# An H3 layer with a long convolution and an MLP on one core: v fetched in the layout of the transform, and a rearranged first MLP chunk

## The chip, the core and the metric

The kernel runs on one core of a Trainium2 chip. A core has TensorE (PE; PEld is its weight load), VectorE (DVE), ScalarE (ACT), GpSimd (POOL) and the DMA queues, most of which SyncE (SP) fills here. Time is device microseconds for one execution. One execution is also taken with the hardware profiler; its trace is what "the profile" means below.

## The reference

S = 2048 positions, D = 640 channels, F = 1728, all float32. `mod` is six vectors of 640 from `silu(c) @ w_mod`.

```
h  = layernorm(q) * (1 + ca) + sa
kv = causal_conv4(k, shift_k) * v              # per channel, four taps
y  = irfft(rfft(kv, 2S) * rfft(ssm_k, 2S))[:S] + kv * ssm_D
x  = q + ga * (h * y)
h  = layernorm(x) * (1 + cb) + sb
out = x + gb * (relu(h @ w1 + b1)**2 @ w2 + b2)
```

The long convolution is per channel, over 4096 points. kv is the only place where v is used.

## The kernel before, in words

The channels are five blocks (b = 0 to 4) of 128. The Fourier transform is done by matmuls: a position n is 64 n + i, with 32 values of n and 64 of i; the tile `pt[b]` holds, for 32 groups g of four channels, x (slot 0, the product kv) and the filter h (slot 1) with (channel within the group, n) on the 128 partitions and i along the row. `unit_a` (L355) transforms over n, `spectrum` (L362) over i, `front` multiplies the spectra on DVE and combines them on POOL, `back` (L422), `unit_t` (L485) and `unit_y` (L496) transform back.

For kv the positions of a channel must lie along a row, while k and v lie in memory with the channels along a row. So `kv_load` fetches k and v in quarters h of 512 positions (rows of 512 bytes) into the tile KV, `kv_k` transposes k on PE (L221) and scales it on ACT (L222), `kv_s` adds the other three taps on DVE (L233), `kv_v` transposes v on PE (L243), `kv_m` multiplies the two on DVE (L250) and writes the result to the scratch tensor `kv_d` in DRAM (L251). `load_x` reads it back in the layout of the transform (L198), `load_h` the filter (L190).

The order of the work is written out by hand: block b has ten front steps FS(b, j) and 18 (the last block 11) back steps GS(b, s); a table says which small functions run after which step, and every engine and queue runs its instructions in the order in which they are written. While block b goes through its steps, the blocks behind it are prepared: kv of block b + 1 or b + 2, the weight rows `wm` of `mod` (L302, scaled on ACT at L306, added on POOL), q's columns `xp` (L444). SP's queue holds all these loads in the same order, and one that waits holds up those behind it. `unit_a(b + 1, 0, ...)`, the x units of the next block, begin at GS(b, 6), for block 1 at GS(0, 10).

After the convolution comes the MLP in eight chunks of 256 positions (n), each in 14 slices f of the hidden width: `mlp_front` (L664), relu and bias on ACT (L696), the square on POOL (L136), `mlp_split` into a high and a low part on ACT and DVE (L131, L142), and three slices later `mlp_back` (L734). During the first chunk `beside(f)` also loads the weights, splits them into high and low parts on ACT and DVE, and ends the statistics of the second layer norm (`stats2`); `gate_rows` (L1142) fetches b2 as a row and multiplies it on POOL by gb. `keep_order` fixes the order of each engine's instructions; what is written after it may be reordered by the scheduler. It is called after the first chunk's slices.

Of the kernel before, what the change touches and what calls it, by code (L numbers as in the profile page):

```python
# [87 lines left out]
def ssm_mlp_kernel(  # L88
# [91 lines left out]
    hsrc = ssm_k.rearrange("(g a) (n i) -> (a n) g i", a=4, i=64)  # L180
    xsrc = kv_d.rearrange("(g a) (n i) -> (a n) g i", a=4, i=64)
# [4 lines left out]

    def load_h(b, n=1):
        w = DG // n
        for i in range(n):
            sp.dma_start(  # L190
                pt[b][:, 1, i * w : (i + 1) * w],
                hsrc[:, b * DG + i * w : b * DG + (i + 1) * w, :],
            )

    def load_x(b, n=1):
        w = DG // n
        for i in range(n):
            sp.dma_start(  # L198
                pt[b][:, 0, i * w : (i + 1) * w],
                xsrc[:, b * DG + i * w : b * DG + (i + 1) * w, :],  # L200
            )
# [12 lines left out]
    def kv_k(b, h, tag="Y"):  # L214
        acc = KACC[h % 2] if b else K0[:, h]
        t = kt[0] = ps.tile(
            [P, 512], F32, tag=tag, name=f"kt_{b}_{h}", bufs=4 if tag == "X" else 2
        )
        kn = KN[h % (4 if b == 0 else 2)]
        for j in range(4):  # L220
            pe.transpose(t[:, j * P : (j + 1) * P], kn[:, 0, j], ident)  # L221
        act.activation(acc, t, AF.Copy, scale=tap[:, b, 0:1])  # L222
        if h < 3:
            copy(act, ktail[:, h % 2, 0:3], t[:, 509:512])

# [11 lines left out]
    def kv_v(b, h, tag="X"):  # L237
# [6 lines left out]
        n = 4 * b + h + 2  # L244
        if 6 <= n < 4 * NB:
            kv_load(n)

    def kv_m(b, h):
        acc = KACC[h % 2] if b else K0[:, h]
        dve.tensor_mul(acc, kt[1], acc)  # L250
        sp.dma_start(kv_d[b * P : (b + 1) * P, h * 512 : (h + 1) * 512], acc)  # L251

# [236 lines left out]
    def unit_y(b, g):  # L489
# [13 lines left out]
        if g % 2:  # L503
            uo = UPt[b][:, :, 16 * (g - 1) : 16 * (g + 1)].rearrange("p l (g d) -> p g l d", d=4)
# [94 lines left out]
    def stats2(l0, l1):  # L599
        for l in range(l0, l1):  # L600
            dve.bn_aggr(mv2[:, l], st2[:, l])
        s = slice(l0, l1)
# [24 lines left out]
    def prep_xt(n, b):  # L627
        if b == 0:
# [12 lines left out]
        )  # L641
        copy(act, XT[n][:, 0, b], f)
# [129 lines left out]
    for a in range(4):  # L772
        (pool if a % 2 else act).dma_start(
            dsm[32 * a : 32 * a + 1, :],
            ssm_D.rearrange("(o g a) -> a o g", a=4, o=1)[a],
        )
    act.dma_start(tap, shift_k.rearrange("(b p) t -> p b t", p=P))
    act.dma_start(cw, cw_d.rearrange("p (r m) -> p r m", r=2))
    act.activation(rs1[:, 0:1], eps_t, AF.Copy)
# [4 lines left out]
    def load_h0(i):  # L784
        sp.dma_start(pt[0][:, 1, 8 * i : 8 * i + 8], hsrc[:, 8 * i : 8 * i + 8, :])
# [14 lines left out]
    unit_a(0, 1, 1)  # L800
    kv_all(1)
    load_gb(1)
    unit_a(0, 1, 2)
    unit_a(0, 1, 3)
    kv_all(2)
# [6 lines left out]
    for i in (2, 3):  # L812
        load_gb(i)
# [4 lines left out]
    for i in range(2):  # L818
# [3 lines left out]
        early_h(0, 2 * i + 1)  # L822
    act.dma_start(ct, c.rearrange("o (b p) -> p (o b)", p=P))
# [23 lines left out]
    def put_kv(b, places, tags="YYYY"):  # L847
        for h, p4 in enumerate(places):
            at(p4[0], kv_k, b, h, tags[h])
            for i, fn in zip(p4[1:], (kv_s, kv_v, kv_m)):  # L850
                at(i, fn, b, h)

# [3 lines left out]
    for j in range(4):  # L856
# [4 lines left out]
        [FS(0, i) for i in (1, 2, 3, 4)],  # L861
        [FS(0, i) for i in (5, 6, 7, 8)],
        [GS(0, i) for i in (0, 1, 1, 2)],
        [GS(0, i) for i in (3, 4, 4, 5)],
    ], "TTYX")
    at(GS(0, 6), load_x, 1, 4)
    at(FS(1, 8), load_x, 2)
    at(GS(1, 16), load_x, 3)
    at(GS(2, 16), load_x, 4)
# [3 lines left out]
        [GS(0, i) for i in (8, 9, 10, 11)],  # L873
        [GS(0, i) for i in (12, 13, 14, 15)],
        [FS(1, i) for i in (0, 1, 2, 3)],
        [FS(1, i) for i in (4, 5, 6, 7)],
    ], "XYTT")
    for b in (3, 4):
        at(GS(b - 2, 0), p_tile, b)
        put_kv(b, [[GS(b - 2, 4 * h + i) for i in range(4)] for h in range(4)])  # L880
        at(GS(b - 2, 1), load_h, b)

# [127 lines left out]

    at(FS(4, 4), gate_load)
    at(GS(4, 5), gate_vector)
# [126 lines left out]
    row1b = sb.tile([P, D], F32, tag="row1", name="gb2row")  # L1139

    def gate_rows():
        sp.dma_start(row1b, b2.rearrange("(o d) -> o d", o=1).to_broadcast([P, D]))  # L1142
        mul(pool, row1b, row1b, row0b)

    def residual(n, i, eng):
        add(eng, X1t[n][:, i], X1t[n][:, i], row1b)

    def beside(f):
        n = min(len(stage), len(ahead) + 2 * f)
        while wn[0] < n:  # L1150
# [9 lines left out]
        if f == 2:  # L1160
            stats2(2, 4)
# [4 lines left out]
        if f in (6, 7, 8):  # L1166
            stats2(4 * f - 20, 4 * f - 16)
        if f == 9:
            stats2_end(4, NL)
        if f == 4:  # L1170
            gate_rows()
# [3 lines left out]
    for i in range(len(seq) + MLAG):  # L1175
# [9 lines left out]
        if i <= last:  # L1185
# [5 lines left out]
            if n == 0:  # L1191
                beside(f)
            if n + 1 < NC:
# [4 lines left out]
                if f >= 8 and f - 8 < NB:  # L1198
                    prep_xt(n + 1, f - 8)
# [28 lines left out]
```

## Time and profile before

| | us |
|---|---|
| median of three timed runs | 727.67 (726.03 to 729.06) |
| the profiled execution | 725.62 |
| its span in the trace | 723.8 |
| prologue until the first x unit of block 0 | 0 to 30.9 |
| convolution with its preparation | 30.9 to 313 |
| MLP, first chunk | 313 to 370 |
| MLP, seven further chunks and the tail | 370 to 723.8 |

The span is the part of the execution that the trace covers; some 2 us lie around it. In a row of the timeline stand the start, the length, the engine, the line, the operation, the tile that is written and those that are read, the count, and in brackets the engine's idle time just before and what ended it. In a row of groups stand the busy time, the mean length and the idle time.

### The profile page before, as it was taken

The page shows a single profiled execution, that of the slowest core. Times are in us where ns is not written, and L with a number is a line of the kernel's source. Part 1 is how long each engine was busy: PE and PEld are TensorE (multiplying, and loading weights), DVE is VectorE, ACT ScalarE, POOL GpSimd, SP SyncE. Part 2 cuts the span into 40 slices and gives each one's busy share as a digit, 9 for nine tenths or more (in the row PEclk, how much of TensorE's full clock was granted, in tenths as well). Part 3 has the DMA queues.
Part 4 walks back from the last instruction along what each step waited for, and adds up shares of the span by engine and source line. Part 5 has one row for each costly group of instructions (what it writes and reads, how often), then busy time and mean ns, then how long its engine had stood idle before and what let it go on. Part 6 is the DMA issues. An engine that isn't in the chain of part 4 may idle for free.

```text
span 723.8 us, 18538 instructions
## 1 busy us (share of the span) xinstructions
PE 694.8 (96%) x7916; PEld 660.5 (91%) x7916; DVE 339.3 (47%) x665; ACT 333.4 (46%) x688; POOL 289.5 (40%) x337
## 2 busy tenths in 40 slices
PE   5899999989999999998999999999999999999996
PEld 5788898879899889887899999999999999999996
DVE  3455674576868779676751231232232312322312
ACT  3535565576885876455543323332333233233221
POOL 1033036147846968733363333342342333243211
PEclk9999999999999999999999999999999999999998
DMA  9697685986355473326401020020020010200001
GB/s 222 180 222 242 165 272 152 266 268 163 103 168 147 108 185 122 118 65 180 137 16 58 1 72 3 1 74 1 1 73 1 37 37 1 74 1 1 38 1 38
DMA packets 88563, 72.62 MB, mean 100 GB/s; under 512 B 19552, under 2 KB 74272, under 8 KB 88480
## 3 DMA queue, kind: packets, MB, share of 16 engines
q1 hardware_dynamic: 86176, 70.83, 34.6%
q8 instruction: 62, 1.02, 0.6%
q10 hardware_dynamic: 2240, 0.60, 0.4%
q14 instruction: 21, 0.17, 0.1%
q0 software_dynamic: 64, 0.00, 0.0%
HBM read 57.01 MB, written 14.42 MB: 99 GB/s over the span
## 4 chain that ended last, share of the span: by engine, by line
PE 81%; DVE 6%; ACT 4%; issue 4%; DMA 3%; POOL 2%; ACTq 0%; DVEq 0%; POOLq 0%; SPq 0%
PE acc L734 24%; PE h L664 22%; PE pa L355 8%; PE x L362 5%; PE y L496 4%; PE qp L422 4%; PE h L362 4%; PE t L485 2%; PE kt L221 1%; PE h L655 1%; PE vt L243 1%; PE xtp L632 1%; DMA wx<-in_cw_dram 1%; DVE KV L233 1%; DVE w_S L142 1%
## 5 line engine op out<-in xcount | busy, mean ns | idle before, releaser
L664 PE MATMUL h<-xt,w_S 128*128 128x256 f32 x1290 | 167.1, 281 | 0.1
L734 PE MATMUL acc<-w_S,hring 128*128 128x320 f32 x960 | 159.4, 314 | 4.6 <-ACT hring L131 3.6
L664 PEld LDWEIGHTS h<-xt,w_S 128*128 128x128 f32 x1290 | 161.5, 190 | 0.3 <-DVE w_S L142 0.3
L142 DVE TENSOR_TENSOR hring<-mtmp,hring 128x256 fp32r<-128x256 f32 x112 | 63.1, 563 | 196.8 <-ACT hring L131 196.8
L136 POOL TENSOR_TENSOR mtmp<-mtmp 128x256 f32<-128x256 f32 x112 | 72.8, 650 | 201.7 <-ACT mtmp L696 186.7
L734 PEld LDWEIGHTS acc<-w_S,hring 128*128 128x128 f32 x960 | 142.9, 189 | 6.9 <-ACT hring L131 4.2
L696 ACT ACTIVATE mtmp<-h,b1t 128x256 f32<-128x256 f32 x104 | 48.9, 471 | 131.1 <-PE h L664 128.1
L131 ACT ACTIVATE hring<-mtmp 128x256 fp32r<-128x256 f32 x112 | 46.7, 417 | 89.2 <-POOL mtmp L136 89.2
L355 PE MATMUL pa<-wx,p 128*64 128x128 f32 x1280 | 83.7, 280 | 3.8 <-DMA wx<-in_cw_dram 2.7
L355 PEld LDWEIGHTS pa<-wx,p 128*64 128x64 f32 x1280 | 70.4, 139 | 10.7 <-issue 7.8
L131 ACT ACTIVATE a<-pa 128x512 f32<-128x512 f32 x80 | 47.7, 599 | 26.5 <-PE pa L355 26.5
L136 DVE TENSOR_TENSOR wx<-x,wx 128x512 f32<-128x512 f32 x64 | 40.9, 683 | 21.0 <-ACT wx L131 8.6
L496 PE MATMUL y<-wx,wx 128*64 128x64 f32 x1280 | 44.6, 223 | 3.1 <-ACT wx L131 2.4
L496 PEld LDWEIGHTS y<-wx,wx 128*64 128x64 f32 x1280 | 41.3, 138 | 6.6 <-ACT wx L131 3.5
L233 DVE SCALAR_TENSOR_TENSOR KV<-kt,tap,KV 128x511 f32<-128x511 f32 (+2 forms) x48 | 35.6, 742 | 20.7 <-ACT ktail L131 19.4
L634 DVE TENSOR_SCALAR we<-xtp,cbs 128x256 f32<-128x256 f32 x35 | 19.0, 542 | 55.0 <-PE xtp L632 55.0
L142 POOL TENSOR_TENSOR we<-wx 128x256 f32<-128x256 f32 x20 | 15.7, 783 | 72.1 <-DVE wx L136 67.3
L139 POOL TENSOR_TENSOR wm<-wm,wm 128x640 f32<-128x640 f32 x20 | 31.8, 1590 | 31.2 <-ACT wm L306 31.1
L362 PE MATMUL x<-a,gb 128*64 128x128 f32 x640 | 41.7, 273 | 0.7 <-ACT a L131 0.7
L142 POOL TENSOR_TENSOR xt<-we,xt 128x256 fp32r<-128x256 f32 x35 | 25.7, 735 | 36.0 <-ACT xt L131 36.0
L362 PEld LDWEIGHTS x<-a,gb 128*64 128x64 f32 x640 | 35.9, 137 | 1.7 <-ACT a L131 0.9
L131 ACT ACTIVATE q<-qp 128x512 f32<-128x512 f32 x39 | 21.2, 595 | 34.8 <-PE qp L422 34.8
(143 smaller groups left out, 1040.0 us busy)
## 6 DMA issues: line engine op xcount, KB each, us to landing
wm<-in_w_mod_dram SPq DMA_DIRECT2D x25, 320.0 KB, 4.8
KV<-in_A_k_dram SPq DMA_DIRECT2D x20, 256.0 KB, 6.0
KV<-in_A_v_dram SPq DMA_DIRECT2D x20, 256.0 KB, 4.3
xp<-in_A_q_dram SPq DMA_DIRECT2D x5, 1024.0 KB, 8.4
out_dram<-x SPq DMA_DIRECT2D x14, 320.0 KB, 2.2
w1s<-in_B_w_dram SPq DMA_DIRECT2D x13, 320.0 KB, 3.7
w2s<-in_B_w_dram SPq DMA_DIRECT2D x13, 320.0 KB, 4.1
kv_d<-KV SPq DMA_DIRECT2D x16, 256.0 KB, 4.1
```

The lines of the kernel that those rows point to most:

```text
L131: act.activation(o, i, AF.Copy)
L136: eng.tensor_mul(o, a, b)
L139: eng.tensor_add(o, a, b)
L142: eng.tensor_sub(o, a, b)
L233: dve.scalar_tensor_tensor(o, x, tap[:, b, t : t + 1], o, op0=ALU.mult, op1=ALU.add)
L355: pe.matmul(t[64 * r : 64 * r + 64, u], w, cw[:, r], start=True, stop=True)
L362: pe.matmul(t[64 * a : 64 * a + 64, s + r], gb[:, g, r, a], AX[b][i][:, 2 * g + a], start=True, stop=True,)
L422: pe.matmul(t[a][:, u], gi[l, 4 * j + u, r], w[r][l, u % 2], start=(r == 0), stop=(r == 1),)
L496: pe.matmul(y[64 * h : 64 * h + 64, 4 * (g % 2) + i], tss[g][:, i, 64 * r : 64 * r + 64], ca[:, r, h], start=(r == 0), stop=(r == 1),)
L664: pe.matmul(hps[n, f][:m], WI[1, f][:, a, b], XT[n][:, x, b], start=(b == 0 and i == 0), stop=(b == NB - 1 and i == 2),)
L696: act.activation(r[:m], h[:m], AF.Relu, bias=b1t[:m, f : f + 1])
L734: pe.matmul(acc[2 * s + i], h[:, a, s * P : (s + 1) * P], w[:, y, i * 320 : (i + 1) * 320], start=(f == 0 and ti == 0), stop=(f == NF - 1 ...
```

## The change

1. For blocks 1 to 4, v is no longer transposed and no longer multiplied before `kv_d`: `kv_d` holds the convolved k alone, `kv_v` is gone for these blocks, and `kv_m` only writes. `v_load` fetches v in four parts j of 16 values of i per block, four DMAs each, in pieces of 32 channels (128 bytes) straight into the transform's layout, into the half of KV where v was; block 1 has four slots, later blocks two. `x_mul` multiplies the tile p by it on DVE, for blocks 2 to 4 one product per part j, before the x units.
2. So that 32 neighbouring channels share a partition row, the channels of a group are now 32 apart in blocks 1 to 4: `by_channel` loads h and x with four DMAs of 32 partitions where one of 128 stood (block 1's x: 16 for four), ssm_D's rows are loaded to match, and y's copy into UP writes with the other stride.
3. The steps in the table move: the taps of kv run a few steps earlier, `load_x` one to three steps earlier, and the v loads and products get steps of their own.
4. Prologue: tap and cw are issued first on ACT; block 0's part of ssm_D goes out from POOL in four pieces, the rest later from ACT; the loads of the table gb stand elsewhere in SP's queue.
5. First MLP chunk: b2's row is loaded at GS(4, 1) and multiplied by gb right after gb's copies; the sums of `stats2` go ahead of the weight splits on DVE, and so do the transposes and scalings of the next chunk's input; `keep_order` is called after the last chunk, so that all chunks run in the written order.

On PE nothing changes but the v transposes and the places of the k transposes among the other matmuls.

```diff
+    def by_channel(src, b, i, dst):
+        w = dst.shape[1]
+        if b == 0:
+            v = src.rearrange("(g a) (n i) -> (a n) g i", a=4, i=64)
+            sp.dma_start(dst, v[:, i * w : (i + 1) * w, :])
+            return
+        for a in range(4):
+            c = b * P + 32 * a + i * w
+            sp.dma_start(
+                dst[32 * a : 32 * a + 32],
+                src[c : c + w, :].rearrange("g (n i) -> n g i", i=64),
+            )
...
-        for w, src in ((0, k), (1, v)):
+        for w, src in ((0, k), (1, v)) if b == 0 else ((0, k),):
             sp.dma_start(t[:, w], src[rows, cols].rearrange("(t p) d -> p t d", p=P))
...
     def kv_m(b, h):
         acc = KACC[h % 2] if b else K0[:, h]
-        dve.tensor_mul(acc, kt[1], acc)
+        if b == 0:
+            dve.tensor_mul(acc, kt[1], acc)
         sp.dma_start(kv_d[b * P : (b + 1) * P, h * 512 : (h + 1) * 512], acc)
+
+    VB = KV[:, 1024:5120].rearrange("p (j w i g) -> p j w i g", j=4, w=2, g=DG)[:, :, 1]
+
+    def v_load(b, j):
+        src = v.rearrange("(n i) d -> n i d", i=64)
+        for a in range(4):
+            c = b * P + 32 * a
+            sp.dma_start(
+                VB[32 * a : 32 * a + 32, j % (4 if b == 1 else 2)],
+                src[:, 16 * j : 16 * j + 16, c : c + 32],
+            )
+
+    def x_mul(b, j):
+        if b == 1:
+            x = pt[b][:, 0, 8 * j : 8 * j + 8].rearrange("p g (j i) -> p g j i", j=4)
+            mul(dve, x, x, VB[:, :, :, 8 * j : 8 * j + 8].rearrange("p j i g -> p g j i"))
+        else:
+            x = pt[b][:, 0, :, 16 * j : 16 * j + 16]
+            mul(dve, x, x, VB[:, j % 2].rearrange("p i g -> p g i"))
...
-            uo = UPt[b][:, :, 16 * (g - 1) : 16 * (g + 1)].rearrange("p l (g d) -> p g l d", d=4)
+            if b == 0:
+                uo = UPt[b][:, :, 16 * (g - 1) : 16 * (g + 1)].rearrange("p l (g d) -> p g l d", d=4)
+            else:
+                uo = UPt[b].rearrange("p l (d g) -> p g l d", d=4)[:, 4 * (g - 1) : 4 * (g + 1)]
...
-    for a in range(4):
-        (pool if a % 2 else act).dma_start(
-            dsm[32 * a : 32 * a + 1, :],
-            ssm_D.rearrange("(o g a) -> a o g", a=4, o=1)[a],
-        )
     act.dma_start(tap, shift_k.rearrange("(b p) t -> p b t", p=P))
     act.dma_start(cw, cw_d.rearrange("p (r m) -> p r m", r=2))
+    for a in range(4):
+        pool.dma_start(
+            dsm[32 * a : 32 * a + 1, 0:32],
+            ssm_D[0:P].rearrange("(o g a) -> a o g", a=4, o=1)[a],
+        )
...
+    put_v(1, [FS(0, i) for i in (3, 4, 6, 7)], [GS(0, i) for i in (8, 9, 10, 11)])
+    at(GS(0, 3), load_x, 1, 4)
+    at(FS(1, 7), load_x, 2)
+    at(GS(1, 15), load_x, 3)
+    at(GS(2, 15), load_x, 4)
...
+    put_v(2, [FS(1, 0), FS(1, 2), FS(1, 9), GS(1, 0)], [FS(1, 9), GS(1, 0), GS(1, 3), GS(1, 4)])
+    put_v(3, [GS(1, 9), GS(1, 11), FS(2, 2), FS(2, 3)], [FS(2, 1), FS(2, 2), FS(2, 6), FS(2, 7)])
+    put_v(4, [GS(2, 9), GS(2, 11), FS(3, 2), FS(3, 3)], [FS(3, 1), FS(3, 2), FS(3, 6), FS(3, 7)])
...
+    def b2_load():
+        row1b[0] = sb.tile([P, D], F32, tag="row1", name="gb2row")
+        sp.dma_start(row1b[0], b2.rearrange("(o d) -> o d", o=1).to_broadcast([P, D]))
...
+    at(GS(4, 1), b2_load)
...
+    mul(pool, row1b[0], row1b[0], row0b)
...
-        if f == 4:
-            gate_rows()
...
-        if i == NF - 1:
-            keep_order()
+    keep_order()
```

(`put_v(b, loads, products)` gives the steps of the four loads and of the four products; in one step the product stands before the load. Before, `load_x` stood at GS(0, 6), FS(1, 8), GS(1, 16) and GS(2, 16).)

More of the change, by code (lines that the diff above doesn't have):

```diff
@@ L224, in kv_k @@
             copy(act, ktail[:, h % 2, 0:3], t[:, 509:512])
+        n = 4 * b + h + 2
+        if b and n < 4 * NB:
+            kv_load(n)
     def kv_s(b, h):
@@ L822, in ssm_mlp_kernel @@
         early_h(0, 2 * i + 1)
+    for a in range(4):
+        act.dma_start(
+            dsm[32 * a : 32 * a + 1, 32:].rearrange("o (c g) -> o c g", g=DG),
+            ssm_D[P:].rearrange("(o c a g) -> a o c g", o=1, a=4, g=DG)[a],
+        )
     act.dma_start(ct, c.rearrange("o (b p) -> p (o b)", p=P))
@@ L1138, in ssm_mlp_kernel @@
     w_tile("KV", 4)
[L1139 to L1143, printed above, removed]
     def residual(n, i, eng):
-        add(eng, X1t[n][:, i], X1t[n][:, i], row1b)
+        add(eng, X1t[n][:, i], X1t[n][:, i], row1b[0])
     def beside(f):
         n = min(len(stage), len(ahead) + 2 * f)
+        if f == 2:
+            stats2_sum(2, 4)
+        if f in (6, 7, 8):
+            stats2_sum(4 * f - 20, 4 * f - 16)
         while wn[0] < n:
@@ L1191, in ssm_mlp_kernel @@
             if n == 0:
+                if f >= 8 and f - 8 < NB:
+                    prep_xt1(n + 1, f - 8)
                 beside(f)
```

69 lines of the change are left out of this document (34 added, 35 removed).

## The prediction

> **What bounds the kernel now.** I read the page's busy line first, then a table of windows that cut the span at its stages. Its columns: length, busy time of PE, PEld, DVE, ACT and POOL with instruction counts, granted PE clock, DMA share, GB/s.
>
> ```profile
> PE 694.8 (96%) x7916; PEld 660.5 (91%) x7916; DVE 339.3 (47%) x665; ACT 333.4 (46%) x688; POOL 289.5 (40%) x337
> ...
> 36.00:96.00 60.00, 58.79 (x966) 51.47 (x963) 36.30 (x78) 30.93 (x58) 11.78 (x18) 1.00 0.81 218
> 96.00:158.00 62.00, 59.33 (x991) 52.75 (x988) 39.96 (x84) 39.52 (x72) 25.50 (x27) 1.00 0.81 231
> 158.00:245.00 87.00, 85.68 (x1455) 78.42 (x1455) 63.25 (x119) 62.74 (x128) 61.06 (x61) 1.00 0.53 144
> 245.00:320.00 75.00, 72.17 (x1221) 65.08 (x1218) 57.15 (x107) 49.09 (x105) 49.77 (x48) 1.00 0.42 120
> ...
> 320.00:369.70 49.70, 44.45 (x308) 41.70 (x307) 35.95 (x69) 25.08 (x53) 19.61 (x20) 0.97 0.48 139
> 369.70:418.80 49.10, 49.10 (x379) 49.10 (x378) 14.01 (x27) 16.94 (x39) 20.60 (x26) 1.00 0.08 28
> ```
>
> The reader is to see two things. From 36 to 320 us, the convolution, PE is busy 275.97 of 284 us: a matmul taken out there is a matmul's time won, if nothing new makes PE wait. From 369.7 us each MLP chunk takes 49.1 us with PE never idle, so nothing is to be won there. The one loose stage in between is the first chunk, idle 49.70 - 44.45 = 5.25 us. The DMA share is 0.81 until 158 us and falls to half after it: that is where more DMA work would hurt.
>
> **The change part by part.**
>
> *v's transposes.* Sixteen groups of four go (blocks 1 to 4; block 0 keeps its own). What one costs PE is the distance to the next instruction's start:
>
> ```profile
> 51.73 0.66 PE L243 MATMUL vt<-ident,KV 128*128 128x128 f32 x4
> 52.32 1.97 PE L362 MATMUL x<-a,gb 128*64 128x128 f32 x32
> ...
> 136.49 0.66 PE L243 MATMUL vt<-ident,KV 128*128 128x128 f32 x4
> 136.98 0.60 PE L485 MATMUL t<-ident,q 128*128 128x128 f32 x4
> ...
> L250 DVE TENSOR_TENSOR KV<-vt,KV x16: 636/677/692, 54.8 to 212.8; 128x512 f32<-128x512 f32 x16
> ```
>
> 0.59 us and 0.49 us, so 16 x 0.49 to 0.59 = 7.8 to 9.4 us; I take **-8.7**. DVE's sixteen products of 512 columns (0.68 us) become sixteen of 512 columns on p's tile: equal in count and size. The new ones read v with a stride of 32 floats, and block 1 to 4's copy of y now writes with such a stride. No row of before shows that stride; between no change and double, 0 to 16 x 0.68 = 11 us of DVE work, beside PE. I take no change, the nearest row. [...]
>
> *The first MLP chunk.* This is the surest term. b2's row is fetched at L1142 behind the weight loads on SP's queue, and POOL, which executes in order, waits for it with the squares of the MLP queued behind:
>
> ```profile
> 333.69 0.42 SPq L1142 DMA_DIRECT2D gb2row<-in_B_b_dram  x1
> ...
> 335.68 1.93 PE L664 MATMUL h<-xt,w_S 128*128 128x256 f32 x15
> ...
> 338.24 1.53 POOL L136 TENSOR_TENSOR gb2row<-gb2row,gbrow 128x640 f32<-128x640 f32 x1 [8.54 <-DMA gb2row<-in_B_b_dram]
> ...
> 340.85 1.10 PE L734 MATMUL acc<-w_S,hring 128*128 128x320 f32 x4 [3.24 <-ACT hring L131]
> ...
> 344.49 1.98 PE L664 MATMUL h<-xt,w_S 128*128 128x256 f32 x15
> ...
> 350.32 0.30 ACT L603 ACTIVATE rs<-mv,eps_t 128x4 f32<-128x4 f32 x1 [2.58 <-DVE mv L601]
> ...
> 376.23 1.95 PE L664 MATMUL h<-xt,w_S 128*128 128x256 f32 x15
> ...
> 379.77 1.94 PE L664 MATMUL h<-xt,w_S 128*128 128x256 f32 x15
> ```
>
> and, from the table of windows, the granted clock right after the stall (the column 0.57):
>
> ```profile
> 341.00:345.00 4.00, 3.75 (x16) 3.35 (x17) 3.67 (x7) 1.70 (x5) 1.61 (x2) 0.57 0.07 15
> ```
>
> From one h group to the next the settled period is 379.77 - 376.23 = 3.54 us; here it is 344.49 - 335.68 = 8.81, so 5.27 us too long: 3.24 idle, most of the rest at a granted clock of 0.57. The change loads the row in the last block and multiplies it before the MLP starts, when POOL has nothing queued. The next thing late is the weight stream (load, high half on ACT, low half on DVE), which kept 3.5 to 4.1 us per f before the stall, so I count **-5.0**. The other moves there (statistics' sums ahead of the weight halves on DVE, the next chunk's transposes ahead of them) cut ACT's waits of the 350.32 kind. What is left to win is the other idle time, 5.25 - 3.24 = 2.0, down to nothing; I take **-1.2**. The order fixed for all chunks moves work on ACT and POOL only, where PE has been busy without a gap: 0, hidden by PE; if that cover fails it shows as idle PE in every chunk.
>
> *The prologue.* ACT now issues tap and cw first:
>
> ```profile
> 1.22 1.26 ACTq L773 DMA_DIRECT2D dsm<-in_A_ssm_D_dram  x2
> ...
> 3.17 0.60 ACTq L778 DMA_DIRECT2D wx<-in_cw_dram  x1
> ...
> 7.89 0.21 POOL L139 TENSOR_TENSOR p<-p,dsm 128x8 f32<-128x8 f32 x1 [5.17 <-DMA dsm<-in_A_ssm_D_dram]
> ...
> 9.45 3.68 PE L355 MATMUL pa<-wx,p 128*64 128x128 f32 x32 [2.73 <-DMA wx<-in_cw_dram]
> ```
>
> cw goes out 1.26 us earlier, but the four pieces of dsm now leave POOL one after another, the last some 1.2 us later than before, and end the wait at about 8.8 us. Four more dsm pieces are issued by ACT ahead of block 0's copies, which costs up to 0.5. Between -1.3 and +0.5; I take **-0.5**.
>
> *v's new loads.* A load of v was 2048 pieces of 512 bytes per block; it is now 8192 of 128 bytes, in 16 DMAs. The rows nearest in kind are the 256-byte loads of h and the 512-byte loads of q (GB/s in forty slices of 43 to 46 us, where h is loaded, and of 244 to 249 us, where q is):
>
> ```profile
> GB/s 225 232 218 218 232 205 246 218 205 218 232 218 205 218 232 218 205 218 232 218 205 218 232 218 205 218 218 218 218 178 178 164 96 96 68 68 68 68 82 55
> ...
> GB/s 102 102 20 102 102 143 164 266 389 397 393 320 283 320 295 233 283 315 348 352 348 348 344 356 336 324 315 283 287 279 299 303 303 283 303 291 279 274 279 312
> ...
> 120.00:158.00 38.00, 35.33 (x611) 31.05 (x608) 22.27 (x50) 27.38 (x51) 10.51 (x8) 1.00 0.91 244
> ```
>
> At 218 GB/s on 16 engines a 256-byte piece takes 256 x 16 / 218 = 18.8 ns of an engine; at about 290, a 512-byte piece 28 ns. A 128-byte piece then costs between 9.4 (by bytes) and 28 ns (as the whole 512-byte row it is cut from); I take 18.8, the nearest size. A block's v is 8192 x 18.8 / 16 = 9.6 us of the engines instead of 2048 x 28 / 16 = 3.6: 6 us more per block, in a queue that is 0.81 to 0.91 full for blocks 1 to 3.
>
> *The new waits.* DVE now multiplies p's tile in order: it waits for x to land, and v's second half may be fetched only when the first products have freed its two slots. For block 2:
>
> ```profile
> 114.70 0.73 DVE L233 SCALAR_TENSOR_TENSOR KV<-kt,tap,KV 128x509 f32<-128x509 f32 x1
> ...
> 119.68 0.34 SPq L251 DMA_DIRECT2D kv_d<-KV  x1
> 122.16 0.69 SPq L198 DMA_DIRECT2D p<-kv_d  x1
> 122.90 4.78 SPq L444 DMA_DIRECT2D xp<-in_A_q_dram  x1
> 127.72 2.30 SPq L302 DMA_DIRECT2D wm<-in_w_mod_dram  x1
> ...
> 135.51 1.05 PE L355 MATMUL pa<-wx,p 128*64 128x128 f32 x16
> ...
> DMA to landing us min/median/max: 3.3/5.7/8.0
> ...
> KV<-in_A_v_dram SPq DMA_DIRECT2D x20, 256.0 KB, 4.3
> ```
>
> (The last two rows: x's loads from issue to landing, and v's, median 4.3.) PE gets to this block's first x unit (135.51 before) about 5.5 us earlier, nine groups and the prologue, at 130. The taps end at 115.4 before, so about 111; the write needs 2.5 us (119.68 to 122.16), so x is asked for at 113.6. Its four loads take SP 4 x 0.69 = 2.8 us, then q's column and a weight row stand in the queue as now (4.78 + 2.30): 123.5. x has landed by about 122 and its first two products free the slots, so eight loads of v follow at some 0.4 us each, until 126.5. Their 4096 pieces need 4.8 us of the engines, so v lands between 123.5 + 4.8 + 2 and 126.5 + 4.3, at 130 to 131, and the last product ends a microsecond later. PE waits 1 to 2.5 us; bounds 0 (9.4 ns a piece) and 6 (28 ns and x at the 8.0 us end). I take **+2.0**. Queued behind DVE's wait are the next block's taps and q's statistics, which have 8 us until PE needs their PSUM buffer.
>
> Block 3 has the same chain with less room, at the start of a block's front:
>
> ```profile
> 157.75 0.38 SPq L251 DMA_DIRECT2D kv_d<-KV  x1
> ...
> 158.49 1.09 PE L362 MATMUL h<-a,gb 128*64 128x128 f32 x16
> ...
> 162.35 1.29 DVE L136 TENSOR_TENSOR wx<-x,wx 128x512 f32<-128x512 f32 x2 [0.46 <-PE x L362]
> ...
> 163.15 0.68 SPq L198 DMA_DIRECT2D p<-kv_d  x1
> ```
>
> Counted from the front's start (158.49), the write goes at -0.7 as now or, without v's product, at -3.4; it needs 5.4 us; x lands 5.7 to 8.0 later, at +7.7 to +12.7. DVE arrives at the product after that of j = 1, at 162.35 + 1.29 - 158.49 = +5.1, and waits 2.6 to 7.6 us with the spectrum products behind it. PE has four PSUM buffers and goes on for some 2.7 us: it loses 0 to 4.9, I take **+1.5**. Block 4's DMA share is half: **+0.5**. Block 1's v is fetched ahead, but its taps move between the front's products on DVE: **+0.5**. ACT and POOL work that waits for weight rows delayed by v: **+1.0**, bounds 0 and 4.
>
> **Sum.** -8.7 - 5.0 - 1.2 - 0.5 = -15.4 of gains; +2.0 + 1.5 + 0.5 + 0.5 + 1.0 = +5.5 of new waits; **-9.9 us**. The profiled execution took 725.62 us (span 723.8), which is below all three timed runs (726.03 to 729.06, median 727.67). So 715.7 on its scale, 717.8 on the median's; I forecast **717.0 us**, nearer to the median's.
>
> **The rivals.** *The cover holds:* v's pieces are cheap and x lands in time; the new waits stay under 1 us in all, 725.6 to 727.7 less 14.5 to 15.4: **about 712**. For it: DVE idles just where block 2's first products stand. Against it: block 3's read is issued 4.7 us after the front starts even now. *The queue fills:* at 28 ns a piece, the 120 to 158 us stage needs 0.91 x 38 = 34.6 us, less five loads of 0.9, plus four of 3.6: 44.5 us of DMA in a stage that PE wants to leave in 36. It runs 8 us late, the gain shrinks to under 2: **about 726**. *The first chunk's wait moves on* to the weight stream and half of that term is lost: **about 720**. *Slower:* one mechanism, the half of v that is fetched on demand. Blocks 2, 3 and 4 each expose 4096 / 16 = 256 pieces per engine between the first product and the last. To end 0.5% slower (3.6 us, about what a measurement of this kernel tells from no change) the three must cost 13 us more than I count, 4.3 each, so 17 ns more a piece: it decides from about 36 ns. At twice the 256-byte row, 37.6 ns, they cost 3 x 4.8 = 14.4 more: **about 732**. Against it: nothing in the trace with pieces of 256 bytes is that slow. [...] The 256-byte rows, at 218 against 290 GB/s, do not show a doubling per piece; no run yet shows 128 bytes.
>
> **How the numbers follow.** Forecast 0.46 (713.5 to 722 on its own), cover holds 0.25, half the first chunk 0.08, the queue fills 0.13, slower 0.08. Faster by over 0.5% (under 724.0) is the first three and a little of the fourth: 0.81; same 0.11; slower 0.08. The range 710 to 726 leaves out the slower rival and the tails.
>
> **What would show it.** Right: no vt groups after block 0; POOL's wait for gb2row gone and the h period near 3.6 us throughout the first chunk, clock 1.00; PE waits of 1 to 4 us at the first x units of block 2 and in the first fronts of blocks 2 and 3 (there x of blocks 3 and 4 is multiplied), released by DVE's product and, behind it, by DMA p or DMA KV. Wrong: a DMA share near 1.0 from 100 to 180 us with wm late on ACT (the queue fills), v's landing times above 8 us, DVE's new product at 1.3 us instead of 0.7, or idle PE in the later chunks.

## The result, and the profile after

The changed kernel takes 737.27 us (median of 4 runs, 735.72 to 740.16) where the kernel before took 728.12 beside it. The ratio over all runs is 1.0134, 95% interval 1.0093 to 1.0176: **slower by 1.3%**. Forecast was 717.0, with a range of 710 to 726. The profiled execution took 740.16 us (span 738.4).

First the busy line of the page and the table of windows, at the same cuts as before (length, busy time of PE, PEld, DVE, ACT, POOL with counts, granted PE clock, DMA share, GB/s):

```profile
PE 694.2 (94%) x7852; PEld 659.6 (89%) x7852; DVE 353.2 (48%) x665; ACT 338.9 (46%) x688; POOL 298.9 (40%) x339
...
36.00:96.00 60.00, 55.52 (x926) 49.25 (x924) 34.51 (x69) 30.40 (x57) 11.74 (x18) 0.97 0.82 179
96.00:158.00 62.00, 54.07 (x900) 47.68 (x897) 41.35 (x84) 35.69 (x65) 22.31 (x25) 1.00 0.96 226
158.00:245.00 87.00, 75.89 (x1229) 68.10 (x1229) 56.01 (x95) 55.59 (x106) 49.10 (x45) 0.92 0.71 147
245.00:320.00 75.00, 69.17 (x1174) 62.62 (x1171) 60.31 (x98) 52.82 (x110) 59.81 (x53) 0.98 0.45 121
320.00:738.40 418.40, 412.74 (x3296) 408.47 (x3295) 146.98 (x292) 148.94 (x325) 152.27 (x186) 1.00 0.14 44
```

PE has 64 matmuls fewer, as planned, yet is busy as long as before (694.2 against 694.8), and idles where it had been full: 29.3 us from 36 to 320, where it was 8.0. The rest of the convolution's loss is the clock column, down to 0.92 in one stage. The whole convolution stands in one pair of windows, from 36 us to the first MLP matmul, before and after.

```profile
36.00:312.68 276.68, 268.88 (x4566) 241.03 (x4562) 193.34 (x380) 178.76 (x352) 145.33 (x149) 1.00 0.64 177
```
```profile
36.00:336.84 300.84, 271.40 (x4490) 241.19 (x4487) 206.40 (x381) 181.69 (x351) 150.28 (x149) 0.97 0.70 162
```

It is 24.2 us longer: 29.4 - 7.8 = 21.6 us more idle, and PE busy 2.5 us more although some 8.7 us of transposes went, so the other matmuls took 11.2 us more. Most of that is the lower clock: added up in windows of 1 us, busy time times the missing part of the clock comes to 8.8 us. After that point the changed kernel gains: 401.6 us to its end where it was 411.1.

The table of PE's waits in this stretch names many releasers and no big one (total, times, longest):

```profile
PE y L523 <- ACT wx L131: 8.4, 3, 5.3
PE y L523 <- ACT up L131: 3.5, 2, 2.2
PE qp L449 <- POOL wx L142: 2.7, 3, 2.2
PE pa L382 <- DVE p L136: 2.5, 1, 2.5
PE y L523 <- DVE KV L242: 2.3, 2, 2.0
PE mr L315 <- POOL wm L139: 2.0, 1, 2.0
PE kt L227 <- issue: 1.8, 1, 1.8
```

Only the fourth is v's product directly. To place the loss by block I use the moment at which ACT copies a block's first q out of PSUM; here the timeline's rows of after:

```profile
107.82 1.08 ACT L131 ACTIVATE q<-qp 128x512 f32<-128x512 f32 x2 [1.96 <-PE qp L449]
...
178.73 1.08 ACT L131 ACTIVATE q<-qp 128x512 f32<-128x512 f32 x2 [2.19 <-PE qp L449]
...
242.97 1.08 ACT L131 ACTIVATE q<-qp 128x512 f32<-128x512 f32 x2 [2.19 <-PE qp L449]
...
301.30 1.09 ACT L131 ACTIVATE q<-qp 128x512 f32<-128x512 f32 x2 [2.05 <-PE qp L449]
```

From one block to the next, in us, read in the same way in every trace (the kernels below are explained with their experiments). A product of a block stands before that block's transform, so stretch 1 to 2 holds block 2's products and the first one or two of block 3's, and stretch 2 to 3 the rest of block 3's and the first of block 4's.

| kernel | ratio to before, 95% | 0 to 1 | 1 to 2 | 2 to 3 | 3 to 4 |
|---|---|---|---|---|---|
| before | 1 | 56.1 | 60.8 | 56.7 | 53.4 |
| after | 1.0134, 1.0093 to 1.0176 | 57.6 | 70.9 | 64.2 | 58.3 |
| no_v (before without v) | 0.9869, 0.9845 to 0.9894 | 52.0 | 58.3 | 56.4 | 53.4 |
| after_noprod | 0.9992, 0.9973 to 1.0012 | 56.5 | 72.5 | 57.2 | 53.5 |
| after_nov | 0.9817, 0.9788 to 0.9845 | 51.0 | 62.0 | 57.4 | 53.5 |
| three_nov | 0.9778, 0.9745 to 0.9812 | 50.9 | 59.8 | 56.3 | 53.4 |

All stretches lose, 1 to 2 most.

### The profile page after: what moved, and what is told of

It is laid out like the page before. It is cut to its first block, busy times and chain, and to the rows that moved or that the text cites. A ratio compares the mean times of both kernels' runs of the same rounds, so it can differ in the third digit from the quotient of the medians.

```text
span 738.4 us, 18493 instructions
## 1 busy us (share of the span) xinstructions
PE 694.2 (94%) x7852; PEld 659.6 (89%) x7852; DVE 353.2 (48%) x665; ACT 338.9 (46%) x688; POOL 298.9 (40%) x339
## 4 chain that ended last, share of the span: by engine, by line
PE 76%; DVE 7%; ACT 5%; DMA 5%; issue 4%; POOL 2%; SPq 1%; ACTq 0%; POOLq 0%; DVEq 0%
PE acc L777 25%; PE h L707 24%; PE pa L382 5%; PE y L523 4%; PE x L389 4%; PE h L389 3%; PE qp L449 3%; DMA kv_d<-KV 3%; PE t L512 2%; DVE KV L242 1%; PE h L698 1%; DMA wm<-in_w_mod_dram 1%; DVE up L136 1%; PE xtp L672 1%; PE eh L389 1%
## 5 line engine op out<-in xcount | busy, mean ns | idle before, releaser
L777 PE MATMUL acc<-w_S,hring 128*128 128x320 f32 x960 | 156.8, 311 | 0.2 <-DVE hring L142 0.2
L142 DVE TENSOR_TENSOR hring<-mtmp,hring 128x256 fp32r<-128x256 f32 x112 | 65.1, 581 | 189.7 <-ACT hring L131 189.6
L523 PE MATMUL y<-wx,wx 128*64 128x64 f32 x1280 | 47.0, 230 | 14.2 <-ACT wx L131 8.4
L523 PEld LDWEIGHTS y<-wx,wx 128*64 128x64 f32 x1280 | 43.6, 144 | 17.7 <-ACT wx L131 9.2
L389 PE MATMUL h<-a,gb 128*64 128x128 f32 x512 | 36.6, 288 | 1.0 <-ACT wx L131 1.0
```

The source lines that it names most:

```text
L142: eng.tensor_sub(o, a, b)
L389: pe.matmul(t[64 * a : 64 * a + 64, s + r], gb[:, g, r, a], AX[b][i][:, 2 * g + a], start=True, stop=True,)
L523: pe.matmul(y[64 * h : 64 * h + 64, 4 * (g % 2) + i], tss[g][:, i, 64 * r : 64 * r + 64], ca[:, r, h], start=(r == 0), stop=(r == 1),)
L777: pe.matmul(acc[2 * s + i], h[:, a, s * P : (s + 1) * P], w[:, y, i * 320 : (i + 1) * 320], start=(f == 0 and ti == 0), stop=(f == NF - 1 ...
```

## Experiments

### The two parts by themselves

**mlp_only** is the kernel before with the first chunk's hunks of the diff alone, **no_mlp** the changed kernel without them.

> The kernel before with the first MLP chunk's edits alone (b2's row fetched and multiplied early, the statistics' sums and the next chunk's transposes moved, the order held to the end). The prediction counted 6.2 us of gain for them (5.0 + 1.2): 722 us. Comparing the two traces by eye, the stretch from the first MLP group to the end is some 9 us shorter after the change (337.24 to 738.4 against 313.09 to 723.8, 401.2 against 410.7): 719 us, if the gain does not hang on the convolution's part. Rival: the wait moves on to the weight stream once the convolution is not late, and half is lost: 724 to 725.

> The changed kernel with the first MLP chunk's edits undone: v's new path and the prologue alone. If the two parts add up, it is the changed kernel plus 9 us, 746; if the convolution's delay covers the wait for b2's row, 738 to 740.

mlp_only 719.24 us, ratio 0.9887 (0.9868 to 0.9907); no_mlp 748.36, 1.0302 (1.0278 to 1.0326). The parts add up roughly: 1.0302 + 0.9887 - 1 = 1.0189, against 1.0134 (1.0093 to 1.0176), a difference at the edge of the uncertainty. v's path and the prologue cost 22 us; the first chunk's edits give 8 on the kernel before and 12 in the changed one. In mlp_only's windows the first chunk is full:

```profile
320.00:369.70 49.70, 49.56 (x379) 49.18 (x378) 39.62 (x79) 28.94 (x62) 23.41 (x25) 1.00 0.45 131
```

### First guesses at v's path: pieces or order

Edits of the changed kernel: **big_v** reads the same bytes in runs of 2 KB, **no_xwait** multiplies v by itself.

```
-                src[:, 16 * j : 16 * j + 16, c : c + 32],
+                v[c : c + 32, 0:512].rearrange("n (i g) -> n i g", g=32),
...
-            mul(dve, x, x, VB[:, j % 2].rearrange("p i g -> p g i"))
+            x = VB[:, j % 2].rearrange("p i g -> p g i")
+        mul(dve, x, x, x)
```

> The changed kernel with each partition's share of a v load read as one run of 2 KB, where it was 16 pieces of 128 bytes (other values of v, so the products are not the reference's); the number of loads, their bytes, places and waits are unchanged. Theory 1, the transfers: the small pieces fill the DMA engines from 36 to 180 us, and x's read, its write and the weight rows come late: most of the loss goes, 718 to 723. Theory 2, the order: DVE stands in order at the product until x has come back from DRAM (24 us of such waits), and the taps, spectrum products and statistics behind it start late; the pieces matter little: 733 to 736.

> The changed kernel with each product of v done on v's own buffer (v times v, of the same shape and stride) and x left as it was read, so that the multiplication by v is left out of the result: DVE waits for v alone, PE waits for x as in the kernel before. Theory 1, the transfers: 733 to 737, since every load is still there. Theory 2, the order: the 24 us of DVE's waits for x go, and with them most of the loss: 716 to 722.

big_v 733.72, 1.0093 (1.0074 to 1.0112); no_xwait 737.58, 1.0153 (1.0135 to 1.0171). Neither theory stands alone: cheap pieces give 3 us, inside the two intervals, and without DVE's wait for x nothing is gained at all. (The products are still done there; this comes back below.)

### The other new costs: reads by 32 partitions, strides

**one_dma** reads h and x again in one DMA of 128 partitions; **contig** copies y as block 0 does and reads v's buffer in order; **three** has both and big_v's edit.

```
-        for a in range(4):
-            c = b * P + 32 * a + i * w
-            sp.dma_start(dst[32 * a : 32 * a + 32], src[c : c + w, :]...)
+        v = src.rearrange("(g a) (n i) -> (a n) g i", a=4, i=64)
+        sp.dma_start(dst, v[:, b * DG + i * w : b * DG + (i + 1) * w, :])
...
-            mul(dve, x, x, VB[:, j % 2].rearrange("p i g -> p g i"))
+            mul(dve, x, x, VC[:, j % 2])
```

> The changed kernel with h and x of blocks 1 to 4 read as before, one DMA over 128 partitions in place of four over 32 (the channels of a block are then in another order than v's, so the products pair wrong values). With the two first theories fallen (smaller pieces of v account for some 3 us, DVE's waits for x for none), theory 3: these reads are dear in the new form. h's load moved 160 GB/s at a DMA share of 0.91 from 36 to 46 us, where before it moved 261 at 1.09, so x and h hold the queue longer, and SP issues four times as many: 725 to 729. Theory 4, the strides (the product of v 1.07 us where it was 0.67, the copy of y 1.05 us on ACT where it was 0.60): 735 to 738, no change.

> The changed kernel with the strides taken out: y copied as in block 0, and v's buffer read in its own order (so channels and times are paired wrongly). Sixteen products of v give back 0.40 us of DVE each, sixteen copies of y 0.45 us of ACT or DVE each. Theory 4, the strides: 726 to 730. Theory 3, the reads of h and x: 734 to 737.

> The changed kernel with all three undone: v read in runs of 2 KB, h and x in one DMA each, no strides (values paired wrongly). What stays of the change is the order: the places of k's, v's and x's loads and of the products, and the wait for x. If the three costs add up to the whole loss: 712 to 716, which is the first chunk's edits and the transposes taken from the kernel before (727 - 8 - 9 = 710), plus the few us of new waits that the prediction counted. If the order itself is what is lost: 722 to 730.

one_dma 733.98, 1.0095 (1.0061 to 1.0128); contig 736.61, 1.0109 (1.0078 to 1.0141); three 724.52, 0.9954 (0.9936 to 0.9971). Big_v, one_dma and contig give 3, 3 and 2 us, none of them told from nothing by itself; together they give 13 us. Three is still 14 us from the 710 that the two gains promise: something else counts too.

### The gain that was there to be had

**no_v** leaves v of blocks 1 to 4 out of the kernel before (`range(4 if b == 0 else 0)` at the transposes, no load, no product).

> The kernel before with v of blocks 1 to 4 neither fetched, nor transposed, nor multiplied (left out of the result); all else at its place. It shows what the change could win at most in the convolution. By the prediction's step, PE time that goes is time won: 727 - 8.7 = 718. Rival: PE's order only moves the wait to ACT's copies and to the weight rows: 722 or more. Less than 716 would say that v's loads or DVE's products were in the way too.

718.36, 0.9869 (0.9845 to 0.9894), 9.5 us, and PE's busy time falls from 694.8 to 685.4: the transposes were worth what the prediction gave them.

### A theory of SP's order that fell

**after_v3_later** changes one line of the changed kernel and leaves nothing out; **three_v3_later**, **three_noxwait** and **three_later_noxwait** put this edit and no_xwait's on three.

```
-    put_v(3, [GS(1, 9), GS(1, 11), FS(2, 2), FS(2, 3)], ...
+    put_v(3, [GS(1, 16), GS(1, 17), FS(2, 2), FS(2, 3)], ...
```

> The changed kernel, still computing the same, with one edit: the first eight loads of block 3's v stand seven and six places later on SP's queue, behind the weight rows of w_mod. Theory 5, SP's order: in this stretch a weight row is fetched when POOL frees its buffer, ACT scales it, POOL adds it, and the next may be fetched. POOL freed buffers at 156.6 and 160.0, but SP issued the rows at 159.91 and 163.72, behind v's loads (154.36 for 3.23 us, 160.34 for 2.03): 7 us late in all, ACT waited in order, PE stood 5.28 us, and the clock was 0.82 to 0.84 for 20 us after (3.4 us more). Without it: 728 to 731. Rival: v then comes late for block 3's first product, DVE waits there, and the time stays within 2 us, 735 to 739.

> The same edit on the kernel with v read in runs of 2 KB, h and x in one DMA each and no strides (values paired wrongly; 724.5 before this edit). There the rows went out 1.7 and 3.5 us after their buffers were free, and PE stood 5.43 us. Theory 5, SP's order: 715 to 718, the stall and the slower clock behind it. Rival: the row is late since all of the stage's transfers are late: 722 to 725.

> The kernel with v read in runs of 2 KB, h and x in one DMA each and no strides, and besides the product done on v's own buffer, x left alone (the multiplication by v is left out). Theory 2, DVE's order, found no gain when the rest was in place; here PE's waits that follow from DVE's waits for x are 1.2 + 1.7 (block 2), 2.2 and 2.1 us (blocks 3 and 4): 716 to 718 if they count now, 723 to 725 if other waits take their place again.

> All of them together: v in runs of 2 KB, h and x in one DMA each, no strides, block 3's first loads of v behind the weight rows, and the product on v's own buffer (the multiplication by v is left out). If transfers, strides, SP's order and DVE's order are the whole loss, this comes to what the two gains give alone, 0.9887 and 0.9869 of the kernel before: 709 to 712. What stays above that has yet another cause.

after_v3_later 738.74, 1.0172 (1.0126 to 1.0218): no gain. three_v3_later 722.25, 0.9934 (0.9914 to 0.9955); three_noxwait 721.71, 0.9929 (0.9909 to 0.9949); three_later_noxwait 721.21, 0.9914 (0.9888 to 0.9940): against three's 0.9954 3 us at most. The stop that I had aimed at became shorter, 3.46 us for 5.28, and the next one came behind it, in the front where block 3's first product now waits for v. PE and DVE in after_v3_later:

```profile
159.65 1.98 PE L523 MATMUL y<-wx,wx 128*64 128x64 f32 x32 [3.46 <-ACT wx L131]
176.80 1.09 PE L389 MATMUL h<-a,gb 128*64 128x128 f32 x16 [2.24 <-DVE wx L136]
...
174.52 1.03 DVE L136 TENSOR_TENSOR p<-p,KV 128x512 f32<-128x512 f32 x1 [5.89 <-DMA KV<-in_A_v_dram]
```

Stretch 1 to 2 takes 67.3 us there instead of 70.9, 2 to 3 69.0 instead of 64.2: the wait moved on, as v came later.

### Taking the products away, and adding them alone

**after_noprod** and **three_noprod** keep v's loads and leave the products out (`x_mul` is empty). **no_v_xwait** goes the other way: no_v, and four products of x with itself for each of blocks 2 to 4 at the change's places.

> The changed kernel without the products of v (left out of the result); v's loads are all still issued, at their places. DVE waits neither for x nor for v, and no buffer of v waits for a product. Theory 8, one wait behind another: DVE stands at block 2's products either for x (until 129.4) or, where that wait is taken away, for the half of v fetched on demand; the next block's taps stand behind, SP stands at their write to DRAM, and the weight rows stand behind that on SP. Taking one of the two waits away leaves the other, so both must go: 722 to 727, what stays being the smaller pieces of v, h and x and the stride of y's copy. Rival, the transfers after all: 732 or more.

> v read in runs of 2 KB, h and x in one DMA each, no strides, and no products of v (left out of the result), v's loads still issued at their places. Theory 8: nothing of the loss is left, 709 to 713 (0.9887 + 0.9869 - 1 of the kernel before is 709). Rival: v's loads by themselves, 64 more issues on SP among weight rows and k's loads, keep it at 718 to 722.

> The kernel before with v left out (718 us before this edit), and one thing added: blocks 2, 3 and 4's x is squared in place on DVE, four products of 512 columns at the places that the change gives them, so that DVE stands in order until x is back from DRAM. No v is loaded, and h and x are read as before. Theory 8: this wait alone makes the next block's taps late, and with them SP's writes and the weight rows: 724 to 729. Rival, DVE's wait is covered: 718 to 720.

after_noprod 726.97, 0.9992 (0.9973 to 1.0012): the products are worth 10 us, nearly all of it in stretches 2 to 3 and 3 to 4, which now take 57.2 and 53.5, close to no_v. Stretch 1 to 2 does not get shorter: 72.5. no_v_xwait 731.27, 1.0041 (1.0020 to 1.0063), 12.5 us more than no_v: stretches 2 to 3 and 3 to 4 go from 56.4 and 53.4 to 61.9 and 57.7, while 1 to 2, with the longest of DVE's waits, stays at 57.7. First DVE's waits at its products (three of them, 17.5 us), then PE's stops behind them, in no_v_xwait:

```profile
DVE p L136 <- DMA p<-kv_d: 17.5, 3, 8.7
```
```profile
163.90 1.79 PE L368 MATMUL h<-a,gb 128*64 128x128 f32 x16 [1.97 <-DVE wx L136]
...
228.81 0.67 PE L428 MATMUL qp<-wx,gi 64*128 64x128 f32 x4 [2.09 <-POOL wx L142]
```

In a front, DVE's spectrum products and POOL's sums stand behind the product. But is it the wait for x, or the product's own time on DVE? Two pairs of kernels differ in the products alone, and in both DVE waits neither for x nor, in blocks 3 and 4, for v. no_xwait has products of 1.2 us on DVE and takes 11.7 us more than after_noprod; stretches 2 to 3 and 3 to 4 take 63.4 and 58.4, which is 6.2 and 4.9 more. three_noxwait has products of 0.68 us and takes 6.0 us more than three_noprod; the two stretches take 59.5 and 56.5, 3.2 and 3.1 more. With the wait for x added, after is no slower than no_xwait, and three is 1.8 us slower than three_noxwait, which is inside the intervals. no_v_xwait, with products of 0.68 us and the wait, loses 5.6 and 4.3 in the two stretches, so there the wait has a part as well. But without the wait the products cost most of what they cost with it in the changed kernel: it is their time on DVE. The front of block 3, where block 4's products now stand, shows why. In the kernel before, DVE is busy there for 12.75 of 13 us, beside a PE that never stops; the products of kv came ahead of that front (the last at 212.82, the front from 215.18). In three_noxwait DVE is busy for 15.88 of 16 us and PE for 14.19. The two windows, two of the new products (no wait in brackets), and PE's stop behind the second:

```profile
218.00:231.00 13.00, 13.00 (x228) 12.42 (x226) 12.75 (x22) 5.09 (x10) 8.28 (x12) 1.00 0.64 177
```
```profile
220.00:236.00 16.00, 14.19 (x248) 13.40 (x244) 15.88 (x25) 5.36 (x10) 9.29 (x12) 1.00 0.68 180
```
```profile
222.93 0.72 DVE L136 TENSOR_TENSOR KV<-KV 128x512 f32<-128x512 f32 x1
...
227.07 0.67 DVE L136 TENSOR_TENSOR KV<-KV 128x512 f32<-128x512 f32 x1
```
```profile
231.61 1.09 PE L382 MATMUL x<-a,gb 128*64 128x128 f32 x16 [1.81 <-DVE wx L136]
```

In the front of block 2, where block 3's products stand, DVE had room before (busy 8.47 of 14 us from 160 to 174), and where that part is lost stays open.

three_noprod 716.68, 0.9847 (0.9819 to 0.9875): some 5 us above the middle of the 709 to 713 of theory 8, and all of it in stretch 1 to 2 (65.1; the others 51.2, 56.3, 53.4). after_noprod's 72.5 there shows where. SP's queue, DVE, ACT and PE:

```profile
128.31 8.75 SPq L267 DMA_DIRECT2D KV<-in_A_v_dram  x8
137.15 0.43 SPq L216 DMA_DIRECT2D KV<-in_A_k_dram  x1
137.63 4.75 SPq L194 DMA_DIRECT2D p<-in_A_ssm_k_dram  x4
142.49 1.42 SPq L258 DMA_DIRECT2D kv_d<-KV  x1
```
```profile
127.17 2.32 DVE L242 SCALAR_TENSOR_TENSOR KV<-kt,tap,KV 128x511 f32<-128x511 f32 x3 [7.21 <-ACT ktail L131]
...
149.73 0.75 DVE L242 SCALAR_TENSOR_TENSOR KV<-kt,tap,KV 128x511 f32<-128x511 f32 x1 [12.30 <-ACT ktail L131]
```
```profile
148.95 0.69 ACT L228 ACTIVATE KV<-kt,tap 128x512 f32<-128x512 f32 x1 [8.06 <-DMA kv_d<-KV]
```
```profile
152.38 1.97 PE L518 MATMUL y<-wx,wx 128*64 128x64 f32 x32 [5.54 <-ACT up L131]
```

The taps of block 3's first slice are done at 129.5 on DVE, but their write to DRAM stands on SP behind eight loads of v (8.75 us, 1.1 us each; the DMA share is 1.04 from 126 to 156 us), k and h, and goes out at 142.49. There are two accumulators for the slices; the third slice needs the first one's, so ACT waits 8.06 us until it has been written out, and behind it on ACT stand the copies of y, so PE stops for 5.54 us. This is the loop that the prediction missed. It is in the changed kernel too (eight loads at 130.52 for 6.12 us, the write at 142.90, ACT's wait 3.57, PE's stop 2.17).

### v's loads taken away

**after_nov** is the changed kernel without v's loads and products for blocks 1 to 4, **three_nov** the same with one DMA for h and x and no strides.

> The changed kernel with v of blocks 1 to 4 neither fetched nor multiplied (left out of the result); h and x read by 32 partitions, y copied with its stride, all places as changed. Without the products alone it took 727.0, and the loss that stayed lay in blocks 1 and 2: 72.5 us from block 1's first q to block 2's, where the kernel before without v takes 58.3. If v's 64 loads (their pieces and their places on SP) are that loss: 712 to 716. If the reads of h and x, the strides or the moved places are: 721 to 725.

> The changed kernel with v of blocks 1 to 4 neither fetched nor multiplied (left out of the result), h and x in one DMA each and no stride (values paired wrongly). With v's loads in runs of 2 KB still issued it took 716.7, and 65.1 us from block 1's first q to block 2's. If it is their 64 places on SP that cost: 709 to 711, and 58 us there. If it is the moved places of k's and x's loads and of the taps: 715 to 717, and 64 to 66 us there.

after_nov 713.34, 0.9817 (0.9788 to 0.9845); three_nov 709.70, 0.9778 (0.9745 to 0.9812). v's loads by themselves cost 0.9992 - 0.9817, 12.7 us, and 5 us even in runs of 2 KB (0.9847 - 0.9778). That is their places on SP, as the chain above shows, together with the moving of their bytes, which no run separates. The moved places of k's and x's loads cost nothing that shows: three_nov is what the two gains give, 0.9887 + 0.9869 - 1 = 0.9756.

### The better kernel

**mlp_pro** is mlp_only with tap and cw first on ACT, D's pieces on POOL, and gb's parts a step earlier.

> The kernel before with the two parts that seem to gain: the first MLP chunk's edits (0.9887 alone) and the prologue's inputs in the change's order, tap and cw first on ACT, D's four pieces on POOL (all of D at once), gb's parts a step earlier. The prediction counted 0.5 us for the prologue, and the changed kernel's first product of block 0 starts 0.86 us earlier than before: 718 to 719 where the first part alone gave 719.2. Rival: the start is not on the path, no difference.

718.54, 0.9883 (0.9864 to 0.9901); it leaves nothing out and beats both kernels. The prologue's part is not told from nothing beside mlp_only's 0.9887.

## Why the prediction was wrong, step by step

The whole loss by subtraction, each row one experiment against the next (a ratio of 0.001 is 0.73 us; the differences carry some 0.003 to 0.005 of uncertainty each):

| step | ratios | us |
|---|---|---|
| products of v on x: wait and work | 1.0134 to 0.9992 | 10.3 |
| v's loads: pieces and places on SP | 0.9992 to 0.9817 | 12.7 |
| h and x by 32 partitions, strides (without v) | 0.9817 to 0.9778 | 2.8, not told from 0 |
| first chunk and transposes, the gains | 0.9778 | -16.1 |

The gains were right, 16.1 us for the 15.4 forecast. What failed is the +5.5 us for all that is new: it cost about 26. Two steps of it were wrong, the price of v's loads on SP (block 2 below) and the products taken as work beside PE (blocks 3 and 4).

- **Transposes, -8.7: right.** no_v shows 9.5 (7.7 to 11.3), with v's loads and products out as well.
- **First chunk, -6.2: right in kind, small in size.** 8.2 (6.8 to 9.6). Of the 9.3 us between the two spans (723.8 and 714.5), 5.5 are idle time and 3.8 PE busy time (694.8 against 691.0 for the same 7916 matmuls). The slow clock, 0.57 from 341 to 345 us and 1.00 in the rest of the chunk, accounts for 3.75 x 0.43 = 1.6 of the 3.8; the other 2.2 stay open. In the changed kernel POOL's product of b2's row is done at 339.37, before PE's next h group at 340.67, and nothing waits for it:

```profile
337.80 1.57 POOL L136 TENSOR_TENSOR gb2row<-gb2row,gbrow 128x640 f32<-128x640 f32 x1 [10.48 <-ACT gbrow L131]
```

- **Prologue, -0.5: not told from nothing.** The first product of block 0 does start 0.86 us earlier (9.45 before):

```profile
8.59 3.68 PE L382 MATMUL pa<-wx,p 128*64 128x128 f32 x32 [1.64 <-POOL p L139]
```

- **v's pieces: dearer than by bytes, cheaper than I took them, and not the main thing.** From 181 to 184 us of after the DMA summary shows v alone:

```profile
DMA packets 2546, 0.32 MB, mean 108 GB/s; under 512 B 2545, under 2 KB 2545, under 8 KB 2545
...
q1 hardware_dynamic: 2545, 0.32, 67.6%
```

0.676 x 3 us x 16 engines / 2545 = 12.7 ns for 128 bytes; I took 18.8. The row that I took it from was misread: in the trace, h's loads of before are not packets of 256 bytes. The summary of its 43 to 46 us counts 564 packets, 993 bytes each in the mean, 13 of them under 512:

```profile
DMA packets 564, 0.56 MB, mean 187 GB/s; under 512 B 13, under 2 KB 564, under 8 KB 564
...
q1 hardware_dynamic: 564, 0.56, 98.0%
```

That is 83 ns a packet. The summaries of 37 to 44 us, where h is loaded, in after (packets, share of 16 engines) and in one_dma, which reads it as before:

```profile
DMA packets 4457, 1.29 MB, mean 184 GB/s; under 512 B 3877, under 2 KB 4456, under 8 KB 4456
...
q1 hardware_dynamic: 4456, 1.27, 107.4%
```
```profile
DMA packets 1746, 1.40 MB, mean 201 GB/s; under 512 B 44, under 2 KB 1745, under 8 KB 1745
...
q1 hardware_dynamic: 1745, 1.39, 90.8%
```

In one_dma a packet has 802 bytes and takes 58 ns; in after, 289 bytes and 27 ns, a third more per byte (other loads share both windows). So the change made h and x dearer as well, and the prediction's sum had no term for that at all: 2.9 us by one_dma, not told from nothing alone, but part of three's 13. No run here separates the size of the packets from the reading by 32 partitions.
- **Strides, 0: the durations were wrong, the sum not.** The products take 1.07 us (before 0.68), ACT's copies of y 0.90 in the mean of strided and plain (before 0.60, all plain); contig moved the time by 1.8 us, inside its interval.

```profile
L136 DVE TENSOR_TENSOR p<-p,KV 128x512 f32<-128x512 f32 x16 | 16.9, 1068 | 26.9 <-DMA p<-kv_d 15.1 <-issue 9.0 <-DMA KV<-in_A_v_dram 2.8
```
```profile
L131 ACT ACTIVATE up<-y 128x512 f32<-128x512 f32 x12 | 10.8, 903 | 8.1 <-PE y L523 4.9 <-issue 3.2
```

- **Block 2, +2.0: the direct wait had the right size, partly by luck; the cost lay elsewhere.** PE waited 2.5 us for the product. But x was asked for at 120.73, not 113.6, and DVE had it at 129.4, not 122; the last product ended at 140.65 and PE came there at 138.2, both some 8 us later than I had worked out. The step that failed is "eight loads of v follow at some 0.4 us each", with nothing counted for what stands behind them on SP. They took 6.12 us (8.75 in after_noprod), and behind them stood the write of the next block's taps, and behind that the accumulator, ACT and PE. I had followed DVE's queue instead, to the next block's taps, "which have 8 us until PE needs their PSUM buffer". That queue was not it: without the products stretch 1 to 2 is no shorter (72.5 against 70.9), with DVE's wait alone it is no longer (57.7 against 58.3), and without v's loads it takes 62.0. It lost 12.6 us to no_v.
- **Block 3, +1.5, and block 4, +0.5: the waits came, the cost was another.** DVE waited 3.6 us for block 3's x, within the 2.6 to 7.6 forecast, and 2.2 for block 4's. Against after_noprod the stretches lost 64.2 - 57.2 = 7.0 and 58.3 - 53.5 = 4.8 us, and no_xwait and three_noxwait show that they lose most of this without any wait. The step that failed is the sentence that the products are "equal in count and size" to those of before, with DVE's work "beside PE" at no cost: their place changed, and in the front of block 3 DVE was already full. Behind DVE's longer front stand POOL's sums, the q after them and, after a stop, the slow clock (0.50 from 252 to 254 us, behind a stop of 2.23 us at the q of 249.96).
- **Block 1, +0.5:** 57.6 in stretch 0 to 1, 56.5 without the products and 51.0 without v's loads as well, so 6.6 us, most of it the loads.
- **ACT waiting for weight rows, +1.0:** ACT waited 4.9 us, PE 5.28 at one stop; but the stop was a meeting of all the delays, and taking its nearest cause away (after_v3_later) won nothing.
- **The rivals.** The time lies beyond all of them. The queue was nearly full (DMA share 0.96 from 96 to 158), but cheap pieces alone gave 3 us. The slower rival had the direction right, not the mechanism: it needed 36 ns a piece, and a piece takes 12.7. Its doubling was an assumption of mine that no run shows: per byte a packet took 0.10 ns at 128, 0.09 at 289, 0.07 at 802 and 0.08 at 993 in the four summaries above, so the small ones are dearer, but half as dear again at most.

## What to carry to other kernels

When work moves to where its data comes back from DRAM, follow each in-order queue past the new wait to everything behind it, and from there to whoever holds the buffers: here SP, ACT and PE formed a chain through a double-buffered accumulator. Work of equal size that moves is not free: look how busy its engine is at the new place (here DVE was busy for 12.75 of 13 us in the kernel before). Loads on an in-order queue count by their places too (v's 64 loads cost 5 us even in runs of 2 KB), and a packet's size is read from a count of packets, not from a tile's shape. If single fixes win nothing, take the whole part away in steps, and time each stage apart, until the rest is what the kernel must do.

## What was not expected of the hardware

The granted clock was about a half for 2 to 5 us after some of PE's stops, and that adds some 40 to 50% to the price of the stops. The windows of after around its 5.28 us stop, and around the stop of 2.36 us at 71.08 (PEclk is the third column from the end):

```profile
164.00:168.00 4.00, 2.88 (x34) 2.57 (x35) 0.43 (x2) 2.85 (x5) 1.54 (x1) 0.50 0.90 244
168.00:172.00 4.00, 4.00 (x49) 2.94 (x50) 1.36 (x3) 2.17 (x3) 1.54 (x1) 0.80 0.93 179
```
```profile
71.00:73.00 2.00, 1.93 (x33) 1.81 (x33) 2.00 (x6) 1.48 (x4) 0.00 (x0) 0.50 0.97 209
73.00:75.00 2.00, 2.00 (x24) 1.67 (x24) 1.93 (x7) 0.60 (x1) 0.00 (x0) 0.74 0.87 242
```

A stop of 2.46 us, which ended at 140.70, left it at 1.00 until 146, so length alone does not decide, and what does, no run here shows. In all the slower matmuls made 11.2 us beside 21.6 us more idle time; 8.8 of them show in the clock.
